# A fused attention and FFN kernel: heads' rows loaded while the chunk runs, the row sums' inverse later, input splits on two engines

## The chip, the cores and the metric

One core of a Trainium2 chip runs the kernel; the other cores do nothing. The metric is the device time of one execution in microseconds (us), as the median of several runs. TensorE is called PE here, its weight load PEld, VectorE DVE, ScalarE ACT, GpSimd POOL, and SP is the engine that only issues transfers.

## The reference

A sequence of 2048 rows of 640 numbers goes through two branches whose sum is gated row by row. Branch A is attention with 32 heads of 20 in 4 chunks of 512 rows: causal softmax inside a chunk, mixed with a read of a memory that the chunks before have filled. Branch B is a gated FFN. Abridged:

```python
g = sigmoid((x * gate_w).sum(-1, keepdims=True))
# A, for each chunk s of 4, 32 heads of 20
p = softmax(qs @ ks.T * 20 ** -0.5 + mask)
a_mem = (phi(qs) @ M) / (phi(qs) @ z + 1e-6)       # phi(t) = t + 1 if t > 0 else exp(t)
o_s = sigmoid(beta) * a_mem + (1 - sigmoid(beta)) * (p @ vs)
M, z = M + phi(ks).T @ vs, z + phi(ks).sum(rows)
a = concat(o_s) @ wo
# B
b = (silu(x @ w1) * (x @ w3)) @ w2                 # 640 -> 1728 -> 640
out = g * a + (1 - g) * b
```

Everything is float32 at the kernel's interface.

## The kernel before

**Numbers.** A float32 operand of a dense product is split into a high half (rounded to the type PE multiplies fast, `fp32r`) and a low half (what is left). `split` makes both: a copy on ACT (L111) and a subtraction on POOL, or on DVE where `lo` says so (L112). A product takes three passes: high by high, high by low, low by high. Queries and keys are cut into three bfloat16 parts each (`qs`, `ks`), which go to DRAM (`qd`, `kd`) and come back per pair of heads as `qst` and `kst`, with 120 rows.

**Attention.** `attention` is a software pipeline over 128 heads (4 chunks of 32). One step has nine places and ten ticks, called slots here. For head j, `s_unit` computes the scores three times over (s_j_0 to s_j_2), and DVE takes the row maxima under the mask (L530, result m). After every second head `max_parts` and `max_rows` cut the maxima into three bfloat16 parts and turn them (L549, result mr), and four ticks later ACT issues the transfer of mr into three more rows of `qst` (L551). Three steps behind, `st_unit` computes the transposed scores with those rows in (t_j_0 to t_j_2), ACT takes the exponential into P (tag P32, 4 buffers) and POOL masks the diagonal (L576). Four steps behind, and for four heads at once, `pv_quad` multiplies by the values (o, L587); the copy `oq` goes to DRAM as `od`, 40 slots from one quad to the next. Row 20 of a head in `od` holds its softmax sums.

**End of a chunk.** After the chunk's last quad (`q == 7`) `o_sums` loads the sums into `rs`; `o_scale` inverts them on DVE (L623 to L628: a reciprocal and five small operations that cut the result into three parts `rp`) and sends them to `rR`; `o_load` loads the heads' rows from `od` into the five blocks of `oall`. `after(n, f)` puts a call n ticks off. `normalize` multiplies: rr is a product of `rR` with a selection matrix (L649), and DVE multiplies `oall` by it and adds the memory's part `gm`.

**Dense work.** Between the attention's slots a hand-written list of jobs runs in segments: q, k and v projections, the memory's read (`memory_read`, eight halves of a product nd and four DVE operations, result gm), FFN up (g, u, result ht) and down (f, added to acc), and the output projection (op). Chunks 0 and 1 go together, then 2 and 3. `braid(a, b, every, skip)` puts one step of b after every `every` steps of a; `chain` puts jobs in a row. Weights come as raw tiles `wr` (2 buffers) and are split into `W` (6 buffers) by `w_load`, `w_split` and `w_step`, which count steps.

**What sets the order.** PE runs in the order in which the program is written. The other engines' order is made by a scheduler from a simulated time line, in which `here` and the pins hold some instructions back. Each engine works its list in order, so an instruction that waits holds everything behind it; the same goes for SP's list of transfers and for the transfers that ACT and POOL issue.

Of the kernel before, what the change touches and what calls it, by code (L numbers as in the profile page):

```python
# [8 lines left out]
F32 = mybir.dt.float32  # L9
# [8 lines left out]
P = 128  # L18
S, D, H, DH, NSEG, L = 2048, 640, 32, 20, 4, 512
F = 1728  # L20
KB = D // P
# [5 lines left out]
NST, NW, NRAW, NHT, NVG, ND = 4, 6, 2, 6, 2, 3  # L27
KR = 6 * DH
LAG_T, LAG_P, NP, AGE = 3, 4, 4, 4
HEADS = [(128 * b // DH, min(H - 1, (128 * b + 127) // DH)) for b in range(KB)]  # L30
PSEG = ((0, 512), (512, 384), (1024, 256), (896, 128))

# [2 lines left out]
def gated_mix(ctx: ExitStack, tc: tile.TileContext, xT, wqk, wv, w13, w2, w2h, wo, beta, out):  # L35
    nc = tc.nc
    cp = ctx.enter_context(tc.tile_pool(name="cp", bufs=1))
    sp = ctx.enter_context(tc.tile_pool(name="sp", bufs=2))
# [58 lines left out]
    here = tc.keep_in_program_order  # L97
    last = {}
# [11 lines left out]
    def split(dst, src, lo=None, pin=lambda ins: ins):  # L110
        pin(nc.scalar.copy(dst[:, 0], src))  # L111
        (lo or nc.gpsimd.tensor_sub)(dst[:, 1], src, dst[:, 0].bitcast(F32))  # L112
# [16 lines left out]
    items, tiles = [], {}  # L129
# [5 lines left out]
    raws, clock = [], dict(step=0, oldest=0, next=0)  # L135

    def w_load():
        k = clock["next"]
        src, n = items[k]
        raw = sp.tile([P, D + 2], F32, tag="wraw", name=f"wr{k}", bufs=NRAW)  # L140
        nc.sync.dma_start(raw[:, :n], src)
        raws.append([k, raw, n, clock["step"], None])
        clock["next"] += 1

    def w_split():
        k, raw, n, _, after = raws.pop(0)
        w = sp.tile([P, 2, D + 2], FR, tag="W", name=f"W{k}", bufs=NW)
        tiles[k] = w
        split(w[:, :, :n], raw[:, :n], lo=nc.vector.tensor_sub if k < 7 else None, pin=behind(after))

    def w_step():


        clock["step"] += 1
        for r in raws:
            if clock["step"] - r[3] == (AGE // 2 if "exp" in last else AGE) and r[0] >= 7:
                r[4] = last.get("exp", last["act"])
        if raws and raws[0][0] < clock["oldest"] + NW and \
                clock["step"] - raws[0][3] >= (AGE if "exp" in last or raws[0][0] < 7 else AGE + 1):
            w_split()  # L160
        if len(raws) < NRAW and clock["next"] < min(len(items), clock["oldest"] + NW + NRAW):
            w_load()

    def w_get(i, oldest=None):
# [9 lines left out]
    Xs, accs = {}, {}  # L174
# [14 lines left out]
    def load_wide(c):  # L189
        for kb in range(KB):  # L190
            nc.sync.dma_start(xraw[c][:, kb], xT[c, :, kb, :])
        for kb in range(KB):
            split(Xs[c][:, :, kb, :], xraw[c][:, kb])
        return
        yield

    def load_raw(c):

        if c == 2:
            wide = big_tile(f"xr{c}")  # L200
            rs = [wide[:, kb * L:(kb + 1) * L] for kb in range(KB)]
        else:
            rs = [t[:, i] for t in (ht_tile([P, 2, L], F32, f"xr{c}_{n}") for n in range(2)) for i in range(2)]
            rs.append(f_tile(f"xr{c}"))
        for kb in range(KB):
            nc.sync.dma_start(rs[kb], xT[c, :, kb, :])
        xraw[c] = rs
        return
        yield

    def split_x(c):
        x_tile(c)
        for kb in range(KB):
            split(Xs[c][:, :, kb, :], xraw[c][kb], lo=nc.vector.tensor_sub if c == 2 or kb % 2 else None, pin=here)
            yield 1

    xraw = {}
# [59 lines left out]
    def memory_read(c):  # L277
        pq = big.pop(("q", c))[:, :KB * L].rearrange("p (b n) -> p b n", b=KB)
        for qb in range(4):
            gm = ht_tile([P, D], F32, f"gm{c}_{qb}")  # L280
            for hf in range(2):
# [3 lines left out]
                for b in range(KB):  # L285
                    a0, a1 = HEADS[b]
                    u0, u1 = max(a0, 16 * hf), min(a1, 16 * hf + 15)
# [110 lines left out]
    def job_read(c):  # L398
        return 5.6, memory_read(c)

    def job_v(cs):
        iv = [w_add(wv[i], D + 2) for i in range(KB)]
        return [(17.8, v_blocks(c, iv, c == cs[-1])) for c in cs]

    def job_q(cs, mb, alloc={}):
        i = w_add(wqk[mb], D)
        return [(3.5, q_block(c, mb, i, alloc.get(c))) for c in cs]
# [173 lines left out]
    def pv_quad(j):  # L581

        ps = pp.tile([P, L], F32, tag="o", name=f"o{j}", bufs=1)
        for kb, (o, n) in enumerate(PSEG):
            for i in range(4):
                u = heads[j + i]
                nc.tensor.matmul(ps[32 * i:32 * i + 32, kb * P:], u["v"][:, kb], u["P32"][:, o:o + n],  # L587
                                 start=kb == 0, stop=kb == 3, skip_group_check=True)
        ot = sp.tile([P, L], F32, tag="oq", name=f"oq{j}", bufs=1)
        nc.scalar.copy(ot, ps)  # L590
        q = j // 4 % 8
        c, h = heads[j]["c"], heads[j]["h"]
        nc.scalar.dma_start(od[c][h:h + 4].rearrange("h e n -> (h e) n"), ot)
        if q == 7:
            after(4 if c < NSEG - 1 else 2, o_sums, c)

    turned = []

    def o_sums(c):
        here(nc.sync.dma_start(rs, od[c][:, DH].rearrange("h (a n) -> h a n", n=P)))  # L600
        after(7 if c < NSEG - 1 else 3, o_scale, c)
        for b in range(KB):
            after(1 + 6 * b if c < NSEG - 1 else 1 + b, o_load, c, b)

    def o_load(c, b):

        if b == 0:
            oall[c] = cp.tile([P, KB, L], F32, tag="oall", name=f"oall{c}", bufs=1)
        f = P * b
        queue = nc.gpsimd if c < NSEG - 1 else nc.sync  # L610
        while f < P * (b + 1):
            h, e = divmod(f, DH)
            n = min(DH - e, P * (b + 1) - f) if e else max((P * (b + 1) - f) // DH * DH, min(DH, P * (b + 1) - f))
            dst = oall[c][f - P * b:f - P * b + n, b]
            if n > DH:
                here(queue.dma_start(dst, od[c][h:h + n // DH, :DH]))
            else:
                here(queue.dma_start(dst, od[c][h, e:e + n]))
            f += n
# [42 lines left out]
    def after(n, f, *a):  # L662
        soon.append([n, f, a])
# [76 lines left out]
    def store(c, qb=None):  # L740
        o = out[0, c * L:(c + 1) * L, :].rearrange("(b p) d -> p b d", p=P)
        for qb in range(4):
            here(nc.gpsimd.dma_start(o[:, qb], accs[c][:, qb]))
            yield 1
# [12 lines left out]
    def job_down(cs, g, last=False):  # L757
        return 2.384 * sum(3 if j < NF else 2 for j in GROUPS[g]), ffn_down(cs, GROUPS[g], plan_down(GROUPS[g]), last)

    def jobs_up(cs, g):  # L760
        return [job_up(cs, j) for j in GROUPS[g]]

    def jobs_group(cs, g):
        return [job_up(cs, j) for j in GROUPS[g]] + [job_down(cs, g)]
# [14 lines left out]
    def chain(jobs):  # L779
        return sum(c for c, _ in jobs), (y for _, g in jobs for y in g)  # L780

    def braid(a, b, every, skip=0, rest=True):

        def gen():
            n = 0
            for y in a[1]:
                yield y
                n += 1
                if n > skip and (n - skip) % every == 0:
                    z = next(b[1], None)  # L790
                    if z is not None:
                        yield z
            if rest:
                yield from b[1]
        return a[0] + b[0], gen()

    A, B = (0, 1), (2, 3)
# [16 lines left out]

    seg = job_q2(A, 3)
    g = jobs_group(A, 0)
    seg += [braid(g[0], job_read(1), 2, 4)] + g[1:] + jobs_group(A, 1) + jobs_up(A, 2)
    segs.append((H + LAG_P + 1, seg))
    d = job_down(A, 2)
    u = job_up(A, GROUPS[3][0])  # L820
    o1, o2 = jobs_oproj(0)
    seg = [d, braid(u, o1, 2), o2] + [job_up(A, j) for j in GROUPS[3][1:]] + [job_down(A, 3)]
    u0, u1 = jobs_up_by_chunk(A, 4)
    seg += [(0, load_raw(2)), (0, load_raw(3))] + u0 + [braid(chain(u1), (0, split_x(2)), 3)]
    seg += [braid(job_down(A, 4), (0, split_x(3)), 3), (0, store(0))]
    seg += job_q(B[:1], 0, {2: big_tile}) + job_v(B)
    kb_, turns, writes = jobs_k(B)
    seg += kb_ + turns[:1] + job_q(B[1:], 0, {3: slot}) + turns[1:] + writes
    segs.append((2 * H - 3, seg))
    seg = job_q(B, 1) + job_q(B, 2)  # L830
    q = job_q2(B, 3)
    r = job_read(2)
    seg += q[:2] + [q[2], braid(q[3], r, 1, 0, False)]
    segs.append((2 * H + LAG_P, seg))
    up = [job_up(B, 0), job_up(B, 1)]
    o1, o2 = jobs_oproj(1)
    r = 0.37 * job_read(3)[0], chain([r, job_read(3)])[1]
    seg = [braid(braid(up[0], r, 2), (0, load_memory(1)), 5, 8), braid(up[1], o1, 2, 2), o2, (0, store(1)), job_up(B, 2), job_down(B, 0), (0, load_memory(2))] + jobs_up(B, 1)
    segs.append((3 * H + LAG_P + 1, seg))
    d = job_down(B, 1)  # L840
    u = job_up(B, GROUPS[2][0])
    o1, o2 = jobs_oproj(2)
    seg = [d, braid(u, o1, 3), o2] + [job_up(B, j) for j in GROUPS[2][1:]]
    seg += [job_down(B, 2), (0, load_memory(3))] + jobs_up(B, 3)
    segs.append((NJ + LAG_P, seg))
    d, u = job_down(B, 3), jobs_up(B, 4)
# [30 lines left out]
    while run:  # L877
# [10 lines left out]
        while credit > 0:  # L888
            d = step(run)
# [62 lines left out]
```

## Time and profile before

| | |
|---|---|
| runs | 1172.35, 1175.51, 1178.13 us; median 1175.51 |
| profiled execution | 1175.76 us, span of its instructions 1174.0 us |
| granted TensorE clock, mean | 0.995 |
| instructions | 19926 |
| DMA | 151.88 MB, mean 129 GB/s |

The page gives busy time and its share of the span for each engine, then the same in 40 slices, the transfers, and the chain of work that ended last, followed back from the last instruction. By that chain 81% of the span is PE, 7% DVE, 5% issue, 4% DMA and 2% POOL. Other views used below are the waits (who waited for whom), the windows (busy time in stretches) and the timelines. A line such as L523 is a line of the kernel before.

### The profile page before, as it was taken

The page shows a single profiled execution, that of the slowest core. Times are in us where ns is not written, and L with a number is a line of the kernel's source. Part 1 is how long each engine was busy: PE and PEld are TensorE (multiplying, and loading weights), DVE is VectorE, ACT ScalarE, POOL GpSimd, SP SyncE. Part 2 cuts the span into 40 slices and gives each one's busy share as a digit, 9 for nine tenths or more (in the row PEclk, how much of TensorE's full clock was granted, in tenths as well). Part 3 has the DMA queues.
Part 4 walks back from the last instruction along what each step waited for, and adds up shares of the span by engine and source line. Part 5 has one row for each costly group of instructions (what it writes and reads, how often), then busy time and mean ns, then how long its engine had stood idle before and what let it go on. Part 6 is the DMA issues. An engine that isn't in the chain of part 4 may idle for free.

```text
span 1174.0 us, 19926 instructions
## 1 busy us (share of the span) xinstructions
PE 1147.3 (98%) x6953; PEld 873.1 (74%) x6953; DVE 676.9 (58%) x2116; ACT 487.7 (42%) x924; POOL 494.6 (42%) x636
## 2 busy tenths in 40 slices
PE   8999999999999999999999988999999999999998
PEld 5978866767767787878876655767768776776888
DVE  5043575466656653674255886866567676663444
ACT  6255344544343234253365633445543344344130
POOL 7065533244245335254175544343445325344250
PEclk9999999999999999999999998999999999999999
DMA  8365733322324225225376865242434324231212
GB/s 282 121 212 208 242 102 94 94 89 83 89 94 131 69 83 152 89 74 178 117 248 222 251 204 162 84 152 91 151 107 127 97 67 134 73 117 53 82 58 90
DMA packets 108097, 151.88 MB, mean 129 GB/s; under 512 B 14244, under 2 KB 71588, under 8 KB 107996
## 3 DMA queue, kind: packets, MB, share of 16 engines
q1 hardware_dynamic: 80908, 112.71, 30.9%
q10 hardware_dynamic: 22080, 27.40, 6.6%
q0 software_dynamic: 5008, 10.50, 2.8%
q8 instruction: 54, 0.88, 0.3%
q14 instruction: 47, 0.39, 0.1%
HBM read 95.25 MB, written 54.53 MB: 128 GB/s over the span
## 4 chain that ended last, share of the span: by engine, by line
PE 81%; DVE 7%; issue 5%; DMA 4%; POOL 2%; ACT 1%; POOLq 0%; SPq 0%; ACTq 0%; DVEq 0%
PE f L478 15%; PE u L225 14%; PE g L225 14%; PE o L587 6%; PE s L523 6%; PE k L225 5%; PE q L225 5%; PE op L724 4%; PE t L562 4%; PE v L325 3%; DVE junk L530 2%; DMA wr<-in_wqk_dram 2%; PE pm L381 1%; PE t L567 1%; DMA od<-oq 1%
## 5 line engine op out<-in xcount | busy, mean ns | idle before, releaser
L530 DVE CUSTOM_DVE_ANT_0 junk<-s,mask 128x128 bf16<-128x128 f32 (+3 forms) x512 | 249.4, 487 | 202.0 <-PE s L523 193.0
L570 ACT ACTIVATE P<-t 128x384 f32<-128x384 f32 (+1 forms) x384 | 201.8, 527 | 343.8 <-PE t L562 106.9
L112 POOL TENSOR_TENSOR W<-wr,W 128x640 fp32r<-128x640 f32 (+1 forms) x126 | 197.6, 1573 | 232.5 <-ACT W L111 224.6
L576 POOL TENSOR_SCALAR_AFFINE_SELECT P<-P 128x256 f32<-128x256 f32 x256 | 106.8, 419 | 329.2 <-ACT P L570 328.6
L225 PE MATMUL g<-X,W 128*128 128x512 f32 x840 | 242.5, 424 | 0.1
L225 PE MATMUL u<-X,W 128*128 128x512 f32 x780 | 228.4, 427 | 0.6 <-DVE oall L650 0.6
L478 PE MATMUL f<-W,ht 128*128 128x320 f32 x1312 | 223.9, 321 | 2.9 <-DVE ft L453 2.2
L478 PEld LDWEIGHTS f<-W,ht 128*128 128x128 f32 x1312 | 199.6, 189 | 10.5 <-DVE ft L453 2.7
L225 PEld LDWEIGHTS g<-X,W 128*128 128x128 f32 x840 | 152.3, 190 | 27.4 <-issue 2.6
L225 PEld LDWEIGHTS u<-X,W 128*128 128x128 f32 x780 | 143.2, 192 | 29.6 <-issue 5.4
L523 PE MATMUL s<-kst,qst 120*128 120x128 bf16 (+3 forms) x512 | 135.6, 305 | 5.2 <-DVE m L530 5.2
L111 ACT CAST W<-wr 128x640 fp32r<-128x640 f32 (+1 forms) x133 | 95.3, 726 | 100.4 <-PE f L478 26.1
L483 DVE SCALAR_TENSOR_TENSOR acc<-f,cgate,acc 128x320 f32<-128x320 f32 x128 | 69.7, 549 | 56.8 <-PE f L478 55.8
L562 PE MATMUL t<-qst,kst 123*128 123x512 bf16 (+1 forms) x256 | 93.5, 365 | 4.9 <-DMA qst<-mr 4.8
L112 POOL TENSOR_TENSOR ht<-ft,ht 128x512 fp32r<-128x512 f32 x52 | 66.9, 1287 | 52.3 <-ACT ht L111 52.3
L225 PE MATMUL q<-X,W 128*128 128x512 f32 x300 | 81.9, 418 | 3.1 <-POOL X L112 1.9
L523 PEld LDWEIGHTS <-qst 120*128 120x128 bf16 x512 | 45.0, 99 | 52.4 <-issue 44.3
L724 PE MATMUL op<-W,oT 128*128 128x320 f32 x480 | 82.3, 323 | 0.0
L225 PE MATMUL k<-X,W 128*128 128x512 f32 x300 | 80.2, 411 | 1.1 <-ACT mt L385 1.1
L587 PE MATMUL o<-P,vg 128*32 128x512 f32 (+3 forms) x1024 | 77.3, 441 | 0.1
L325 PE MATMUL v<-W,X 128*128 128x320 f32 (+1 forms) x480 | 75.9, 317 | 0.0
L724 PEld LDWEIGHTS op<-W,oT 128*128 128x128 f32 x480 | 73.7, 190 | 1.5
(114 smaller groups left out, 1250.0 us busy)
## 6 DMA issues: line engine op xcount, KB each, us to landing
wr<-in_w_dram SPq DMA_DIRECT2D x80, 320.0 KB
qst<-qd SPq DMA_DIRECT2D x64, 240.0 KB
kst<-kd SPq DMA_DIRECT2D x64, 240.0 KB
od<-oq ACTq DMA_DIRECT2D x32, 256.0 KB
qd<-qs ACTq DMA_DIRECT2D x20, 384.0 KB
kd<-ks SPq DMA_DIRECT2D x20, 384.0 KB
wr<-in_wqk_dram SPq DMA_DIRECT2D x21, 320.0 KB
wr<-in_wo_dram SPq DMA_DIRECT2D x20, 320.0 KB
```

Source lines behind the costliest of these rows:

```text
L111: pin(nc.scalar.copy(dst[:, 0], src))
L112: (lo or nc.gpsimd.tensor_sub)(dst[:, 1], src, dst[:, 0].bitcast(F32))
L225: nc.tensor.matmul(ps, w[:, a, kb * P:(kb + 1) * P], x[:, b, kb, :], start=n == 0, stop=n == 14)
L325: nc.tensor.matmul(ps[:, :n1 - n0], x[:, a, kb, lb * P:(lb + 1) * P], wvt[kb][:, b, n0:n1], start=n == 0, stop=n == 14)
L478: nc.tensor.matmul(ps[:, :320], a, b, start=n == 0, stop=n == len(ms) - 1)
L523: nc.tensor.matmul(ps[:, o:o + n], q[:KR, qb * P:(qb + 1) * P], k[:KR, :n], start=qb != 1, stop=qb != 0, skip_group_check=True)
L530: nc.vector.tensor_tensor_reduce(out=junk[:, :n], in0=ps[:, o:o + n], in1=mask[:, L - n:], scale=1.0, scalar=-3.0e38, op0=ALU.add, op1=ALU ...
L562: nc.tensor.matmul(ps[:, :n], k[:KR + 3, t * P:(t + 1) * P], q[:KR + 3, t * P:], start=True, stop=True)
L570: last["exp"] = nc.scalar.activation(P32[:, o:o + n], src, AF.Exp, scale=SCALE)
L576: nc.gpsimd.affine_select(d, d, pattern=[[0, 2], [1, P]], base=0, channel_multiplier=-1, compare_op=ALU.is_ge, fill=0.0)
L587: nc.tensor.matmul(ps[32 * i:32 * i + 32, kb * P:], u["v"][:, kb], u["P32"][:, o:o + n], start=kb == 0, stop=kb == 3, skip_group_check=True)
L724: nc.tensor.matmul(ps[:, :320], oT[0][:, qb % 2, a, kb * P:(kb + 1) * P], ws[kb][:, b, 320 * hf:320 * hf + 320], start=n == 0, stop=n == 14)
```

## The change

It does five things. The heads' rows are loaded block by block after quads 4, 5 and 6 of a chunk (two blocks after the last of these), 8 ticks after each, and only the last block after the sums; in the last chunk too, where those loads move from SP to POOL. The sums are loaded 6 ticks after the last quad (4 before) and inverted 16 ticks later (7 before), except in the last chunk. The low halves of X1, X2 and X3 are shared by POOL and DVE in turn (before: X1 on POOL, X2 on DVE, X3 in turn), and the splits of X2 and X3 are spread over more jobs. Weights 2 to 5 are loaded at the head into P's tiles, which are free then, at fixed steps; weights' splits wait two steps longer before attention. The memory's reads are spread: of chunk 1 over the first two FFN up jobs, of chunk 2 over the last two q jobs, with four of eight halves and not five ahead of the segment's end.

```diff
+EARLY = range(2, 6)
+OUT = {4: (0,), 5: (1,), 6: (2, 3)}
...
     def w_load():
-        raw = sp.tile([P, D + 2], F32, tag="wraw", name=f"wr{k}", bufs=NRAW)
+        if k in EARLY:
+            raw = sp.tile([P, 1280], F32, tag="P32", name=f"wr{k}", bufs=NP)
+        else:
+            raw = sp.tile([P, D + 2], F32, tag="wraw", name=f"wr{k}", bufs=NRAW)
...
     def w_step():
-            if clock["step"] - r[3] == (AGE // 2 if "exp" in last else AGE) and r[0] >= 7:
+            if clock["step"] - r[3] == (AGE // 2 if "exp" in last else AGE + 2) and r[0] >= 7:
...
-        if raws and raws[0][0] < clock["oldest"] + NW and \
-                clock["step"] - raws[0][3] >= (AGE if "exp" in last or raws[0][0] < 7 else AGE + 1):
+        if raws and raws[0][0] in EARLY:
+            if clock["step"] >= 6 + 2 * raws[0][0]:
+                w_split()
+        elif raws and raws[0][0] < clock["oldest"] + NW and \
+                clock["step"] - raws[0][3] >= (AGE if "exp" in last or raws[0][0] < 7 else AGE + 3):
             w_split()
-        if len(raws) < NRAW and clock["next"] < min(len(items), clock["oldest"] + NW + NRAW):
+        if sum(r[0] not in EARLY for r in raws) < NRAW and clock["next"] < min(len(items), clock["oldest"] + NW + NRAW):
             w_load()
...
     def load_wide(c):
             nc.sync.dma_start(xraw[c][:, kb], xT[c, :, kb, :])
+        for _ in EARLY:
+            w_load()
         for kb in range(KB):
-            split(Xs[c][:, :, kb, :], xraw[c][:, kb])
+            split(Xs[c][:, :, kb, :], xraw[c][:, kb], lo=nc.vector.tensor_sub if kb % 2 else None)
...
     def split_x(c):
-            split(Xs[c][:, :, kb, :], xraw[c][kb], lo=nc.vector.tensor_sub if c == 2 or kb % 2 else None, pin=here)
+            split(Xs[c][:, :, kb, :], xraw[c][kb], lo=nc.vector.tensor_sub if kb % 2 else None, pin=here)
...
     def pv_quad(j):
+        for b in OUT.get(q, ()):
+            after(8, o_load, c, b)
         if q == 7:
-            after(4 if c < NSEG - 1 else 2, o_sums, c)
+            after(6 if c < NSEG - 1 else 2, o_sums, c)
...
     def o_sums(c):
-        after(7 if c < NSEG - 1 else 3, o_scale, c)
-        for b in range(KB):
-            after(1 + 6 * b if c < NSEG - 1 else 1 + b, o_load, c, b)
+        after(16 if c < NSEG - 1 else 3, o_scale, c)
+        if c == NSEG - 1:
+            o_load(c, KB - 1)
+        else:
+            after(6, o_load, c, KB - 1)
...
     def o_load(c, b):
-        queue = nc.gpsimd if c < NSEG - 1 else nc.sync
+        queue = nc.gpsimd if (c, b) != (NSEG - 1, KB - 1) else nc.sync
...
-    seg += [braid(g[0], job_read(1), 2, 4)] + g[1:] + jobs_group(A, 1) + jobs_up(A, 2)
+    seg += [braid(chain(g[:2]), job_read(1), 3, 4)] + g[2:] + jobs_group(A, 1) + jobs_up(A, 2)
...
-    seg += [(0, load_raw(2)), (0, load_raw(3))] + u0 + [braid(chain(u1), (0, split_x(2)), 3)]
-    seg += [braid(job_down(A, 4), (0, split_x(3)), 3), (0, store(0))]
-    seg += job_q(B[:1], 0, {2: big_tile}) + job_v(B)
+    x2, x3 = split_x(2), split_x(3)
+    seg += [(0, load_raw(2)), (0, load_raw(3))] + u0 + [braid(chain(u1), (0, x2), 4, 0, False)]
+    d = job_down(A, 4)
+    q = job_q(B[:1], 0, {2: big_tile})
+    seg += [braid(chain([braid(d, (0, x2), 4), (0, store(0))] + q), (0, x3), 4, 6)] + job_v(B)
...
-    seg += q[:2] + [q[2], braid(q[3], r, 1, 0, False)]
+    seg += q[:2] + [braid(chain(q[2:]), r, 2, 2, False)]
```

In the built programs the change shows in the order of the engines other than PE above all. Numbers behind a name are buffers; lines of the changed kernel lie 2 to 16 further down.

DVE at the turn from chunk 1 to chunk 2, before: `rs` is the sums' tile, `junk` and `m68` the maximum of a score tile of heads 68 and 69, `nd_r` part of a memory read, `fu2_0` of the FFN.

```order
L447 SCALAR_TENSOR_TENSOR fu2_0_7630<-ft2_0_7629,g2_0_7521 128x512
L623 RECIPROCAL rs_101<-rs_101 128x128
L530 ISA junk_7654,m68_7330<-s68_2_7652,mask_89 128x512
L530 ISA m68_7330 128x1
L296 TENSOR_SCALAR nd_r_7660<-nd2_3_1_7656 128x16
L624 TENSOR_SCALAR rs_101<-rs_101,cR_99 128x128
L530 ISA junk_7684,m68_7330<-s69_0_7681,mask_89 128x128
L530 ISA m68_7330 128x1
L297 RECIPROCAL nd_r_7660<-nd_r_7660 128x16
L625 CAST rp_102<-rs_101 128x128
```

And in the changed kernel:

```order
L540 ISA junk_7699,m68_7342<-s69_1_7697,mask_89 128x384
L540 ISA m68_7342 128x1
L463 SCALAR_TENSOR_TENSOR ft2_0_7620<-fu2_0_7621,u2_0_7632 128x512
L637 RECIPROCAL rs_101<-rs_101 128x128
L540 ISA junk_7723,m68_7342<-s69_2_7721,mask_89 128x512
L540 ISA m68_7342 128x1
L306 TENSOR_SCALAR nd_r_7740<-nd3_0_0_7736 128x16
L638 TENSOR_SCALAR rs_101<-rs_101,cR_99 128x128
L550 CAST ns0_104<-m68_7342 128x8
L307 RECIPROCAL nd_r_7740<-nd_r_7740 128x16
L639 CAST rp_102<-rs_101 128x128
L551 TENSOR_TENSOR nm_7725<-m68_7342,ns0_104 128x8
```

The inverse has moved from ahead of s68_2 to behind s69_1, so its small operations now lie among those that make `ns` and mr of heads 68 and 69.

POOL in the same stretch, before; the transfers fill chunk 1's `oall`.

```order
L576 AFFINE_SELECT P63_7433<-P63_7433 128x2x128
L112 TENSOR_TENSOR W82_7525<-wr82_7185,W82_7525 128x640
L616 DMA oall1_7587<-od1_81 120x1x512
L618 DMA oall1_7587<-od1_81 8x512
L576 AFFINE_SELECT P63_7433<-P63_7433 128x256
L261 TENSOR_TENSOR qs3_4_7476<-qs3_4_t_7481,qs3_4_7476 128x512
L505 MEMSET vg72_7677 128x4x12
L618 DMA oall1_7587<-od1_81 4x512
L616 DMA oall1_7587<-od1_81 120x1x512
L618 DMA oall1_7587<-od1_81 4x512
L576 AFFINE_SELECT P64_7513<-P64_7513 128x2x128
```

And in the changed kernel, where blocks 2 and 3 stand ahead of P61 (block 0 stands behind P52, block 1 behind P56, block 4 behind P64):

```order
L586 AFFINE_SELECT P60_7193<-P60_7193 128x2x128
L586 AFFINE_SELECT P60_7193<-P60_7193 128x256
L632 DMA oall1_6451<-od1_81 4x512
L630 DMA oall1_6451<-od1_81 120x1x512
L632 DMA oall1_6451<-od1_81 4x512
L632 DMA oall1_6451<-od1_81 16x512
L630 DMA oall1_6451<-od1_81 100x1x512
L632 DMA oall1_6451<-od1_81 12x512
L271 TENSOR_TENSOR qs2_3_7253<-qs2_3_t_7258,qs2_3_7253 128x512
L586 AFFINE_SELECT P61_7290<-P61_7290 128x2x128
```

Four of the five blocks have left the stretch behind P63; they now wait on POOL for the quads that wrote them.

POOL at the head, before: X1 is chunk 1's input, all five low halves on POOL.

```order
L112 TENSOR_TENSOR X1_110<-xr1_111,X1_110 128x512
L311 MEMSET V0_317 128x128
L112 TENSOR_TENSOR X1_110<-xr1_111,X1_110 128x512 x2
L261 TENSOR_TENSOR qs0_0_184<-qs0_0_t_186,qs0_0_184 128x512
L112 TENSOR_TENSOR X1_110<-xr1_111,X1_110 128x512 x2
L261 TENSOR_TENSOR qs0_1_242<-qs0_1_t_244,qs0_1_242 128x512
```

And in the changed kernel; the other two are on DVE, behind the low half of W2:

```order
L321 MEMSET V0_317 128x128
L114 TENSOR_TENSOR X1_110<-xr1_111,X1_110 128x512 x2
L271 TENSOR_TENSOR qs0_0_192<-qs0_0_t_194,qs0_0_192 128x512
L114 TENSOR_TENSOR X1_110<-xr1_111,X1_110 128x512
L321 MEMSET V1_473 128x128
L271 TENSOR_TENSOR qs0_1_235<-qs0_1_t_237,qs0_1_235 128x512
```

POOL is through with X1 after three subtractions, one q part earlier than before.

## Prediction

> **What bounds the kernel now.** I read the page's engine table first, then its row of granted clock over 40 slices, the waits of PE, the windows around the largest of them, and last the chain and the timelines of the engines that PE waits for.
>
> ```profile
> PE 1147.3 (98%) x6953; PEld 873.1 (74%) x6953; DVE 676.9 (58%) x2116; ACT 487.7 (42%) x924; POOL 494.6 (42%) x636
> PEclk9999999999999999999999998999999999999999
> ```
>
> PE's waits, by what it waited for (us in total, times, longest):
>
> ```profile
> PE s L523 <- DVE m L530: 5.2, 6, 3.0
> PE t L562 <- DMA qst<-mr: 4.8, 1, 4.8
> PE f L478 <- DVE ft L453: 2.2, 2, 1.3
> PE k L225 <- ACT mt L385: 1.1, 1, 1.1
> ```
>
> PE is busy for 98% of the span, so the change can only win back idle time of PE and time at a low clock; it removes no matmul. The clock falls in one slice of 40, number 25 (from about 704 us), so I looked there first. The four waits shown are 13.3 us. Single stretches of the dip:
>
> ```profile
> 672.00:692.00 20.00, 18.86 (x129) 12.73 (x127) 19.26 (x75) 9.32 (x19) 12.25 (x19) 1.00 0.77 243
> 692.00:720.00 28.00, 19.96 (x115) 12.78 (x115) 15.01 (x62) 5.65 (x11) 9.74 (x16) 0.82 0.52 160
> 720.00:744.00 24.00, 23.73 (x159) 15.84 (x155) 20.51 (x75) 9.87 (x19) 7.90 (x13) 1.00 0.35 109
> ...
> 696.00:700.00 4.00, 1.13 (x3) 0.94 (x3) 2.69 (x13) 0.00 (x0) 0.00 (x0) 0.81 0.56 155
> 700.00:704.00 4.00, 4.00 (x21) 2.65 (x20) 3.86 (x15) 1.50 (x3) 0.81 (x2) 0.77 0.34 111
> 712.00:716.00 4.00, 1.65 (x4) 1.03 (x4) 0.00 (x0) 0.00 (x0) 0.91 (x2) 0.51 1.02 328
> 716.00:720.00 4.00, 4.00 (x35) 1.29 (x34) 0.56 (x2) 0.00 (x0) 0.00 (x0) 0.63 0.07 28
> ```
>
> After the window's length come PE, weight loads, DVE, ACT, POOL, the granted clock, the DMA share. This is the turn from chunk 1 to chunk 2. PE idles 28 - 19.96 = 8.04 us in the middle stretch. Where the clock is short it is at half: (0.19 + 0.23) x 4 x 2 = 3.4 us around 700, with PE busy about 3.0 of it, and (0.49 + 0.37) x 4 x 2 = 6.9 us around 715, with PE busy about 4.6. Half of that busy time is lost: 1.5 + 2.3 = 3.8 us. How it came about:
>
> ```profile
> 687.13 6.41 DMA od<-oq
> 697.31 0.95 DVE L623 RECIPROCAL rs<-rs 128x128 f32<-128x128 f32 x1 [4.63 <-DMA rs<-od]
> 698.87 0.48 PE L523 MATMUL s<-kst,qst 120*128 120x384 bf16 x1 [3.05 <-DVE m L530]
> 701.98 0.39 PE L523 MATMUL s<-kst,qst 120*128 120x512 bf16 x1
> 703.18 0.68 DVE L530 CUSTOM_DVE_ANT_0 junk<-s,mask 128x512 bf16<-128x512 f32 x1
> 707.90 6.40 DMA qst<-mr
> 714.35 0.61 PE L562 MATMUL t<-qst,kst 123*128 123x512 bf16 x1 [4.81 <-DMA qst<-mr]
> ...
> 750.24 1.94 DMA qst<-mr
> ```
>
> The last quad of chunk 1 lands in od at 693.5, its row sums in rs at 697.3. DVE had come to the reciprocal 4.63 us before and stood there, with the maxima of the next scores behind it, so PE stood 3.05 us. Late maxima gave a late mr, whose transfer took 6.40 us beside the row loads, and PE stood 4.81 us more.
>
> **The change, part by part.** (a) The reciprocal. The row-sum load is put off from 4 to 6 slots after the quad, the inverse from 7 to 16 after that. On DVE it moves from ahead of s68_2 to behind s69_1 and ft2_0, as the rows of the order show: the maxima of s68_2, s69_0 and s69_1 (0.68 us and less, about 2.2 together), ft (another 0.6) and two halves of the memory read now run first, some 5 us of DVE work. That covers the 4.63. On SP the row-sum load stands in the queue until od has landed, with the next heads' loads behind it; two slots later it stands there less. The 3.05 goes (ends: 0 and -3.05; I take -3.05) and the clock loss behind it, -1.5 (0 to -1.5).
>
> (b) The second stall. The six DVE operations of the inverse now stand in the chain from s69_2 to mr, or right ahead of it:
>
> ```profile
> L628 DVE TENSOR_TENSOR rp<-rs,rp x4: 281/289/1328, 375.0 to 1099.7; 128x128 bf16<-128x128 f32 x4
> ```
>
> In the trace mr left 707.90 - 703.18 = 4.72 us after DVE began s69_2's maximum, and DVE began 1.2 us after PE's row. Five operations of 0.29 or less add about 1.3: 7.2 us. From s69_2 to where t68_0 would have started PE needs 714.35 - 4.81 - 701.98 = 7.56 us. That leaves 0.4 us for the transfer, which takes between 1.94 (quiet) and 6.40 (DMA share about 1). Of the five blocks of rows, which POOL issued behind P63 to P66, four now come before P61 and the last behind P64, so less is under way and I put it at 2.4, nearer the quiet row: the wait falls from 4.81 to 2.0, -2.8 (ends: +1.2 with 6.4 us, and -4.81). A wait under 3.05 should not halve the clock: -2.3 (0 to -2.3). [...]
>
> (c) DVE's load there. The same work is 19.26 + 15.01 + 20.51 = 54.8 us from 672 to 744, and PE at full clock without its 9.45 us of idle needs 72 - 9.45 - 3.8 = 58.8: DVE is 93% loaded. One of the memory-read halves goes ahead of 672, but DVE also loses its rest during the stall (0.56 us busy in 712 to 720). From 672 to 692, at 96%, PE lost 6% (1.14 of 20). At 4% of 58.8 PE loses 2.4 us in small waits, where it now loses 9.45 - 3.05 - 4.81 = 1.6 beside the two stalls: +0.8 (from -1.6 to +1.9).
>
> (d) Head: X1's low halves shared.
>
> ```profile
> 16.04 3.71 POOL L112 TENSOR_TENSOR X<-xr,X 128x512 fp32r<-128x512 f32 x2
> 9.63 0.69 DVE L112 TENSOR_TENSOR X<-xr,X 128x512 fp32r<-128x512 f32 x1 [0.22 <-ACT X L111]
> 17.96 0.96 PE L225 MATMUL q<-X,W 128*128 128x512 f32 x3 [1.03 <-POOL X L112]
> 19.80 4.20 PE L225 MATMUL q<-X,W 128*128 128x512 f32 x17 [0.87 <-POOL X L112]
> 23.84 35.85 PE L325 MATMUL v<-W,X 128*128 128x320 f32 x240
> ```
>
> POOL's last pair runs to 19.75, and PE waits 1.03 + 0.87. Two of five go to DVE at 0.69; POOL does three and is through near 16. The wait goes: -1.9 (0 to -1.9). The early loads of four weights into P's tiles gain nothing by themselves: all 240 v matmuls ran without a wait. They stand behind X1's loads on SP, so they delay nothing that PE waits for (0; up to +1, the 0.87 again, if X1 came late).
>
> (e) to (h), smaller places. Rows of the timelines (start, length, instruction, in brackets the idle time ahead of it and what ended it) and three of the chain:
>
> ```profile
> 72.81 0.72 ACT L111 CAST W<-wr 128x640 fp32r<-128x640 f32 x1 [2.31 <-DMA wr<-in_wqk_dram]
> 149.98 0.96 PE L291 MATMUL nd<-Ms,pq 128*128 128x84 f32 x6 [0.71 <-DVE gm L299]
> 161.13 0.38 PE L523 MATMUL s<-kst,qst 120*128 120x512 bf16 x1 [0.56 <-DVE m L530]
> 371.10 0.95 DVE L623 RECIPROCAL rs<-rs 128x128 f32<-128x128 f32 x1 [2.17 <-DMA rs<-od]
> 374.22 2.92 PE L478 MATMUL f<-W,ht 128*128 128x320 f32 x18 [0.86 <-DVE ft L453]
> 396.89 0.23 PE rr L649
> 399.14 2.29 PE o L587 x32
> 444.27 2.29 PE o L587 x32
> 519.15 1.29 POOL L112 TENSOR_TENSOR X<-xr,X 128x512 fp32r<-128x512 f32 x1
> 519.23 1.24 DVE L542 CAST ns<-nm 128x8 bf16<-128x8 f32 x1
> 521.33 1.00 PE L478 MATMUL f<-W,ht 128*128 128x320 f32 x5 [1.32 <-DVE ft L453]
> ```
>
> (e) In the k blocks a cast on ACT, for a weight needed much later, waits 2.31 for its load with mt's copy behind it. The later split puts it behind mt but ahead of the next k copy: half of PE's 1.1 us, -0.5 (0 to -1.1). (f) Chunk 1's memory read is spread over two FFN blocks instead of one: half of 0.71 + 0.56, -0.7 (0 to -1.3). (g) At the turn from chunk 0 DVE waits 2.17 and PE 0.86; the inverse moves behind ft: -0.8 (0 to -0.9). The inverse comes 2 + 9 slots later; two quads, 40 slots apart, start 45.1 us apart here, so that is about 12 us, and the inverse ends near 387. Its first reader, rr, stands at 396.9, and rR's three loads, now behind one weight load on SP, have 9 us to land: 0. (h) X2's low halves go from DVE alone to DVE and POOL, X3's later: DVE saves one of 0.69 ahead of ft, but POOL's X still lies beside it, and beside such a one a cast took 1.24: -0.5 (0 to -1.3). [...] (i) The early row loads on POOL, the last chunk's among them (formerly SP's): the same number of issues, covered by POOL's idle time (58%); 0, but see the third rival. One memory read moves over a segment's border, which shifts PE's later rows by a step without adding any; 0 either way. PE's rows at the end are the same.
>
> The sum: -3.05 - 1.5 - 2.8 - 2.3 + 0.8 - 1.9 - 0.5 - 0.7 - 0.8 - 0.5 = -13.25 us. The profiled execution took 1175.76 us (span 1174.0 and 1.76 around it), so 1162.5; the median of the three runs, 1175.51, lies 0.25 below it.
>
> **The rivals.** First: t68_0 still waits whole. Its slack of 0.4 us speaks for it, the removed row loads against. The wait of 4.81 and the half clock behind it stay: 1162.5 + 2.8 + 2.3 = 1167.6.
>
> Second: the turn is bound by DVE, and the stalls only changed their name. For it speaks the 93%; against it, that PE lost only 0.27 us from 720 to 744 at 85%. Then (a) to (c), 8.85 us, are not won: 1171.4, which is no change.
>
> Third, slower: the row loads of quads 4 to 6 block POOL's queue.
>
> ```profile
> 854.71 2.29 PE o L587 x32
> 877.40 2.29 PE o L587 x32
> ```
>
> Quads are 22.7 us and 40 slots apart, so the load comes 8 x 0.57 = 4.5 us after its quad, while od took 6.41 us to land in a busy stretch. POOL may so stand some 2 us at each of 12 places (three quads of four chunks), with P's masks, the weights' and ht's low halves behind it. That the masked tiles are read only when their own quad comes, up to 22.7 us later, speaks against it. It decides from 13.25 + 5.9 = 19.15 us, or 1.6 us of PE at each place: 1175.76 + 5.9 = 1181.7 and more.
>
> **How the numbers follow.** The forecast has 0.68, the rivals 0.18, 0.09 and 0.05. A change of under 0.5% (5.9 us) can't be told from none: the three runs alone lie that far apart. Faster: 0.68 + 0.18, less 0.03 for the part of the first rival that falls short of 1169.6: 0.83; same 0.09 + 0.03 = 0.12; slower 0.05. The range: every term at its best gives -19.8 us or 1156.0, which needs all of them at once, and I stop at 1157; above, it takes in the first rival with 2.6 us for small waits: 1170. The second and third, 0.14, are left out.
>
> **What will show it.** (a) is right if DVE has no wait for rs of over 0.5 us at the turns of chunks 0 and 1, wrong if one of 2 us is there. (b) if PE's longest wait for mr is under 3 us and the clock row has no low slice. (c) if PE's waits for DVE from 670 to 735 are 2 to 3 us in all. (d) if PE waits no more for POOL X and v starts near 22 instead of 23.8. (f) to (h) by the three rows above. What would make it wrong: a new stall of 3 us or more at the turn, with a half clock behind it, or POOL waiting for od with PE behind it.

## The result and the profile after

| | before | changed |
|---|---|---|
| runs (us) | 1172.35 to 1178.13, median 1175.81 | 1162.19 to 1163.30, median 1163.26 |
| ratio | | 0.9893, 95% interval 0.9868 to 0.9919 |
| profiled execution, span | 1175.76, 1174.0 | 1163.27, 1161.6 |

The forecast was 1162.5. The page of the changed kernel, its engine table and its row of granted clock, and then the largest of PE's waits behind its first matmuls (total, times, longest):

```profile
PE 1142.8 (98%) x6953; PEld 872.6 (75%) x6953; DVE 674.8 (58%) x2115; ACT 487.3 (42%) x924; POOL 499.6 (43%) x648
PEclk9999999999999999999999999999999999999999
```

```profile
PE t L572 <- DMA qst<-mr: 3.1, 3, 1.7
PE s L533 <- DVE m L540: 1.7, 4, 0.6
PE k L235 <- ACT mt L395: 1.2, 2, 1.0
PE f L488 <- DVE ft L463: 1.1, 1, 1.1
PE nd L301 <- DVE gm L309: 1.1, 2, 0.7
```

The low slice of the clock is gone and no wait is over 1.7 us. Single rows of the turn and of the places where PE now waits, from the timelines:

```profile
375.88 0.94 DVE L637 RECIPROCAL rs<-rs 128x128 f32<-128x128 f32 x1
693.17 0.94 DVE L637 RECIPROCAL rs<-rs 128x128 f32<-128x128 f32 x1
699.41 0.76 ACTq L561 DMA_DIRECT2D qst<-mr  x1
701.52 0.39 PE L572 MATMUL t<-qst,kst 123*128 123x512 bf16 x1
21.33 4.89 PE L335 MATMUL v<-W,X 128*128 128x320 f32 x32
```

DVE does not wait for rs at the turns of chunks 0 and 1 (no bracket), mr of heads 68 and 69 is there after 2.11 us instead of 6.40, t68_0 starts without a wait of its own, and v starts at 21.33 instead of 23.84. The windows of the turn (length, then PE, weight loads, DVE, ACT, POOL, clock, DMA share):

```profile
664.00:684.00 20.00, 18.70 (x127) 12.95 (x125) 17.38 (x64) 10.98 (x21) 9.77 (x14) 1.00 0.83 273
684.00:712.00 28.00, 26.91 (x179) 19.08 (x179) 23.90 (x105) 11.15 (x22) 10.84 (x18) 1.00 0.62 180
712.00:740.00 28.00, 26.71 (x165) 17.07 (x164) 23.41 (x79) 11.93 (x23) 8.56 (x15) 1.00 0.38 110
```

PE idles 76 - 72.32 = 3.7 us there in small waits, all of them for DVE. PE's lead, the start of the same PE row in the trace of before less that in the trace of the changed kernel:

| place | before | changed | lead |
|---|---|---|---|
| after the k blocks | 113.57 | 110.66 | 2.91 |
| after chunk 1's read | 200.19 | 196.50 | 3.69 |
| after the turn from chunk 0 | 374.62 | 369.79 | 4.83 |
| before t58_0 | 644.91 | 639.36 | 5.55 |
| after t58_0 | 645.60 | 641.33 | 4.27 |
| before chunk 1's turn | 679.54 | 675.26 | 4.28 |
| after it | 734.74 | 721.06 | 13.68 |
| after t80_0 | 785.18 | 772.93 | 12.25 |
| last matmul | 1169.99 | 1157.30 | 12.69 |

So 9.40 us come from the turn, 5.5 from the small places and the head, and two new waits, at t58_0 and t80_0, take back 1.3 and 1.4.

### The profile page after: what moved, and what is told of

Read it like the earlier page. It is cut to its first block, busy times and chain, and to the rows that moved or that the text cites. A ratio compares the mean times of both kernels' runs of the same rounds, so it can differ in the third digit from the quotient of the medians.

```text
span 1161.6 us, 19926 instructions
## 1 busy us (share of the span) xinstructions
PE 1142.8 (98%) x6953; PEld 872.6 (75%) x6953; DVE 674.8 (58%) x2115; ACT 487.3 (42%) x924; POOL 499.6 (43%) x648
## 4 chain that ended last, share of the span: by engine, by line
PE 88%; DVE 6%; DMA 2%; issue 2%; ACT 1%; POOL 0%; SPq 0%; POOLq 0%; ACTq 0%; DVEq 0%
PE f L488 16%; PE g L235 16%; PE u L235 15%; PE o L597 6%; PE v L335 6%; PE s L533 6%; PE q L235 5%; PE k L235 5%; PE op L738 4%; PE t L572 4%; DVE junk L540 1%; PE pm L391 1%; PE nd L301 1%; PE t L577 1%; DMA qst<-mr 1%
## 5 line engine op out<-in xcount | busy, mean ns | idle before, releaser
L235 PE MATMUL u<-X,W 128*128 128x512 f32 x780 | 225.9, 425 | 0.6 <-DVE nd_r L306 0.6
```

Of the source, the lines that this page charges most:

```text
L235: nc.tensor.matmul(ps, w[:, a, kb * P:(kb + 1) * P], x[:, b, kb, :], start=n == 0, stop=n == 14)
```

## The experiments

Three edits touch the turn: the inverse put off (I), the rows early (R), chunk 2's memory read spread (M). The rest (head, chunk 1's read, weights' steps, splits of X2 and X3, the last chunk's rows) is called H.

| run | has | median, range (us) | ratio to before, interval |
|---|---|---|---|
| changed | I R M H | 1163.26, 1162.19 to 1163.30 | 0.9893, 0.9868 to 0.9919 |
| e1 | I M H | 1165.49, 1165.25 to 1167.43 | 0.9916, 0.9901 to 0.9931 |
| e2 | R M H | 1164.34, 1164.22 to 1164.63 | 0.9903, 0.9888 to 0.9918 |
| e3 | M H | 1166.73, 1165.49 to 1167.18 | 0.9924, 0.9908 to 0.9941 |
| e6 | I R H | 1164.84, 1163.04 to 1166.09 | 0.9906, 0.9891 to 0.9921 |
| e9 | H | 1170.79, 1169.10 to 1171.57 | 0.9959, 0.9945 to 0.9972 |
| b1 | I | 1172.98, 1169.72 to 1176.95 | 0.9980, 0.9967 to 0.9993 |
| b2 | R | 1165.02, 1164.31 to 1166.77 | 0.9914, 0.9897 to 0.9932 |
| b3 | M | 1168.92, 1167.51 to 1170.18 | 0.9941, 0.9922 to 0.9961 |
| e12 | R H | 1159.82, 1159.41 to 1161.51 | 0.9880, 0.9862 to 0.9898 |
| e13 | R H, later block | 1160.12, 1159.44 to 1161.96 | 0.9880, 0.9864 to 0.9896 |
| e5 | all, X1's low halves on POOL | 1165.56, 1163.47 to 1166.08 | 0.9921, 0.9904 to 0.9937 |
| e4 | all, no early weights | 1164.28, 1163.67 to 1166.37 | 0.9916, 0.9899 to 0.9933 |

The kernel before ran beside each set: 1175.62 beside e1 to e6, 1175.58 beside e9 to b3, 1173.54 beside the last four.

**e1, rows late.** In the changed kernel:

```diff
-        for b in OUT.get(q, ()):
+        for b in OUT.get(q, ()) if c == NSEG - 1 else ():
...
-            after(6, o_load, c, KB - 1)
+            for b in range(KB):
+                after(1 + 6 * b, o_load, c, b)
```

> The changed kernel with the row loads of chunks 0 to 2 put back behind the last quad (POOL issues them 1, 7, 13, 19, 25 ticks after the sums' load); the inverse stays put off. Theory A (two causes: the inverse made the first stall, the row loads beside mr the second): no PE wait of 3 us for the maxima of s69, but mr of heads 68 and 69, which leaves about 6.8 us after s69_2, takes 5 to 6.4 us again where it took 2.11, so PE waits 3.5 to 5 us at t68_0 and may lose 0 to 2.3 us more to a half clock; the wait of 1.11 us at t58_0, beside block 0's load, goes. Time 1163.3 + 3.5 to 5 + 0 to 2.3 - 1.1 = 1165.7 to 1169.5. Theory B (the inverse alone was the cause, the second stall only its echo): no wait over 1 us at t68_0, time 1162 to 1163.5.

The wait came back, with a half clock behind it (mean granted clock 0.997 in e1, 1.000 in the changed kernel), but smaller than expected:

```profile
697.81 0.76 ACTq L561 DMA_DIRECT2D qst<-mr  x1
703.00 0.39 PE L572 MATMUL t<-qst,kst 123*128 123x512 bf16 x1 [2.68 <-DMA qst<-mr]
```

The transfer took 5.2 us where it took 2.11. The wait at t58_0 was gone. Theory B falls.

**e2, inverse early.**

```diff
-            after(6 if c < NSEG - 1 else 2, o_sums, c)
+            after(4 if c < NSEG - 1 else 2, o_sums, c)
...
-        after(16 if c < NSEG - 1 else 3, o_scale, c)
+        after(7 if c < NSEG - 1 else 3, o_scale, c)
```

> The changed kernel with the sums' load 4 ticks after the last quad and the inverse 7 ticks after that, as before; the rows stay early. Theory A: od still lands some 6 us after its quad and the sums 3 to 4 us later, so DVE stands 3 to 5 us at the reciprocal in the turn from chunk 1, PE waits 2 to 3 us for maxima with about 1.5 us of half clock, and 0.9 us at the turn from chunk 0; mr of heads 68 and 69 stays near 2 us and t68_0 waits under 1 us. Time 1163.3 + 2 to 3 + 0 to 1.5 + 0.9 = 1166 to 1168.7. Theory C (the row loads alone were the cause: with them gone the sums land in time): DVE's wait for rs is under 1 us, time 1163 to 1164.5.

Theory A was wrong here. With the rows early, DVE hardly stands at the early inverse:

```profile
687.91 0.95 DVE L637 RECIPROCAL rs<-rs 128x128 f32<-128x128 f32 x1 [0.71 <-DMA rs<-od]
```

So it was the row loads that had made the sums late, as theory C says.

**e3, both.**

> Both of the above: the end of a chunk as before, the rest (head, memory reads, splits) as changed. Theory A: the two stalls and the half clocks come back, which were 9.5 us in the trace from 676 to 720, and 1.1 us at the turn from chunk 0; the wait at t58_0 (1.11) goes: 1163.3 + 9.5 + 1.1 - 1.1 = 1172.8, and the two single undoings need not add up, since a late mr is worse beside the rows. If the rest of the change had carried more than it seems, the time would be under 1169.

6 us better than expected: DVE stood 3.06 us for rs where it had stood 4.63, PE lost 0.60, 0.67 and 0.49 in place of 3.05, and mr took 3.2 us. Something outside I and R carried part of the turn.

**e6, chunk 2's read as before.**

```diff
-    seg += q[:2] + [braid(chain(q[2:]), r, 2, 2, False)]
+    seg += q[:2] + [q[2], braid(q[3], r, 1, 0, False)]
```

> The changed kernel with chunk 2's memory read as before (one half after each step of the last q job, five of eight halves ahead of the segment's end). Theory A: the new PE wait of 1.69 us at t80_0 comes from PE's order, which now has three matmuls less (27 and not 30 dense ones, 1.3 us) between s81_2 and t80_0 and so asks for mr earlier; with the old order it is under 0.5 us, and the turn loses 0 to 1 us to DVE. Time 1163.3 - 1.4 + 0 to 1 = 1161.9 to 1162.9. Rival: the wait comes from the transfer or from DVE and stays over 1 us; time 1163.3 or more.

Half right. The wait at t80_0 is gone, so PE's order made it. But t68_0 waits again, although the rows are early:

```profile
693.89 1.22 DVE L639 CAST rp<-rs 128x128 bf16<-128x128 f32 x1
699.56 0.75 ACTq L561 DMA_DIRECT2D qst<-mr  x1
703.46 0.61 PE L572 MATMUL t<-qst,kst 123*128 123x512 bf16 x1 [3.28 <-DMA qst<-mr]
```

mr left 7.45 us after s69_2 (at 692.11; 6.86 in the changed kernel, 5.92 before): the put-off inverse lies in its chain, as the prediction's step (b) had it. Its transfer took 3.90 us, and no row load was beside it, but 0.82 MB of another queue's loads (packets, MB, share of the 16 engines from 699.56 to 703.46; in the changed kernel 0.05 MB on that queue beside mr):

```profile
q1 hardware_dynamic: 657, 0.82, 68.2%
```

**e9, all three undone.** The diffs of e1, e2 and e6 together.

> The changed kernel with all three edits that touch the turn from chunk 1 undone: inverse early, rows late and chunk 2's memory read as before; only the head, chunk 1's memory read, the weights' steps and the splits of X2 and X3 stay changed. Theory D (the two stalls are one chain, and any of the three edits breaks most of it, so the single undoings add up to less than the whole): both stalls come back with their half clocks, PE waits 2 us or more for maxima and 3 us or more at t68_0. The head and the small places are 2.74 + 0.16 + 0.79 + 0.7 = 4.4 us by PE's lead in the traces, so 1175.6 - 4.4 = 1171.2, from 1170 to 1173. If the edits were independent, the undoings would add: 1166.7 + 1.6 = 1168.3 or less.

1170.8, and both stalls are back:

```profile
697.09 0.48 PE L533 MATMUL s<-kst,qst 120*128 120x384 bf16 x1 [3.11 <-DVE m L540]
711.50 0.39 PE L572 MATMUL t<-qst,kst 123*128 123x512 bf16 x1 [2.44 <-DMA qst<-mr]
```

The second is shorter than expected. H is worth 4.8 us, and the three edits of the turn 7.5 together, while e1, e2 and e6 lose 2.2, 1.1 and 1.6 (4.9): they overlap.

**b1, b2, b3: one edit alone, in the kernel before.** The same lines as above, the other way round: b1 has 6 and 16 ticks, b2 `OUT` for chunks 0 to 2 and the last block 6 ticks after the sums' load, b3 the braid over `q[2:]`.

> The kernel before with the inverse alone put off (sums' load 6 ticks after the last quad, inverse 16 after that). By the prediction's step (a) DVE no longer stands for rs and PE's 3.05 with its 1.5 of half clock and 0.9 at the turn from chunk 0 go; by its step (b) the inverse's small operations then lie in mr's chain, mr leaves 6.6 to 7.4 us after s69_2 and takes 5 to 6.4 us beside the rows, so the wait at t68_0 stays at 4 to 6 us with its half clock: 1175.6 - 3.05 - 1.5 - 0.9 + 0 to 1 = 1170.2 to 1171.2. Theory D's strongest form (the first stall is what makes the second): the second goes as well, 1175.6 - 9.65 - 0.9 = 1165.

> The kernel before with the row loads of chunks 0 to 2 alone put early (blocks 0 to 3 behind quads 4 to 6, the last 6 ticks after the sums' load). Step (b) of the prediction alone: t68_0's wait of 4.81 falls to 0 to 1 and its 2.3 of half clock goes, while the first stall of 3.05 with 1.5 stays: 1175.6 - 4.3 - 2.3 + 1.1 (the new wait at t58_0 beside block 0) = 1170.1. Theory D: od and the sums land sooner too, DVE stands under 2.5 us, PE's first stall is under 1 us and keeps its clock: another 2 + 1.5 less, 1166.6.

> The kernel before with chunk 2's memory read alone spread over the last two q jobs (four halves ahead of the segment's end in place of five). The prediction gave this edit nothing. With inverse and rows as before it was worth 1171.2 - 1166.7 = 4.5 us in the changed kernel, if that estimate of the rest holds: 1175.6 - 4.5 = 1171.1, with DVE's wait for rs near 3 us, PE's first stall 1 to 1.5 us in place of 3.05, t68_0's wait under 1.5 in place of 4.81, and a new wait of 1 to 1.7 us at t80_0. By the prediction's step: 1175.6.

b1 gains 2.6 us, less than either theory said. DVE did not stand, but mr left 7.98 us after s69_2 and t68_0 waited longer than before:

```profile
705.54 0.76 ACTq L551 DMA_DIRECT2D qst<-mr  x1
711.53 0.61 PE L562 MATMUL t<-qst,kst 123*128 123x512 bf16 x1 [5.91 <-DMA qst<-mr]
```

b2 gains 10.6 us, more than theory D said: no stall is left at the turn (DVE stands 0.59 us for rs, PE 0.19 at t68_0). Three rows of b2's chain that ended last, then the same of before (od's row of before stands in the prediction), b3, e9 and e12 (start, time to landing, transfer):

```profile
686.60 3.81 DMA od<-oq
690.42 2.35 DMA rs<-od
702.89 1.93 DMA qst<-mr
```

```profile
693.56 3.73 DMA rs<-od
```

```profile
688.09 6.04 DMA od<-oq
694.15 2.41 DMA rs<-od
705.65 3.64 DMA qst<-mr
```

```profile
685.29 6.45 DMA od<-oq
691.76 3.75 DMA rs<-od
706.48 4.97 DMA qst<-mr
```

```profile
681.61 3.89 DMA od<-oq
685.52 2.32 DMA rs<-od
```

SP's load of the sums waits for od, so every trace gives od's time. At this turn it is 6.0 to 6.5 us in before, e3, e9 and b3, and 3.2 to 4.0 in the eight traces with the rows early. But it is as short in b1 (issued at 686.44, 3.95) and e1 (3.81), where the rows are late:

```profile
690.41 0.55 SPq L600 DMA_DIRECT2D rs<-od  x1
```

The late row loads count from the sums' load, so I alone puts them off by two ticks as well, and most of them then come behind od. What moved on POOL's queue, q0, during od, in before, b1 and b2 (packets, MB, share of the 16 engines):

```profile
q0 software_dynamic: 631, 0.76, 40.0%
q0 software_dynamic: 231, 0.08, 19.4%
q0 software_dynamic: 18, 0.01, 2.7%
```

In the four slow traces it was 0.60 to 0.76 MB, in the ten others at most 0.13: od was late for the row loads. So b1 is not the inverse alone; it also took the row loads off od. The row loads lie beside mr too (5.2 us in e1), but other loads alone also stretch it (3.90 in e6).

b3 gains 6.7 us where the prediction gave that edit 0 and the estimate was 4.5. There od is nearly as slow as before (6.04), but the sums' load takes 2.41 us and not 3.73. Beside it in before lay a load that POOL issues for the memory's read; in b3 that load comes behind the sums (before, then b3):

```profile
693.44 0.59 POOL L640 DMA_DIRECT2D gm<-gd  x1 [0.63 <-PE nd L291]
697.20 0.59 POOL L640 DMA_DIRECT2D gm<-gd  x1 [0.19 <-PE t L562]
```

It is the same in e9 (3.75, the load beside it) and e3 (2.58, behind it). The shift also gives PE three more dense matmuls (36, 33 before) between the last quad and s69_0, and again three (36, 33) from s69_2 to t68_0, so it asks later for what was late. How much of the 6.7 us each of these carries was not isolated.

**e12, e13: the rows and H, without the other two.** e2's and e6's diffs together; e13 also has:

```diff
-            after(8, o_load, c, b)
+            after(18 if b == 0 else 8, o_load, c, b)
```

> The changed kernel with the inverse early and chunk 2's memory read as before, but the row loads early: the edit that alone gave 10.6 us at the turn, beside the head and the small places. Theory E (the late row loads were the common root: they lay beside the last quad's od, its sums and mr; with them gone the other two edits cost more than they win, since the put-off inverse lies in mr's chain and the shifted read brings t80_0's wait of 1.69): 1165.0 - (1175.6 - 1170.8 = 4.8) = 1160.2, from 1159.5 to 1161.5, that is 2 to 3 us faster than the changed kernel. If the two edits help beside the rows as their single undoings say (1.1 and 1.6 us), the time is 1163.3 + 2.7 = 1166.

> The same with block 0 loaded 18 and not 8 ticks after quad 4. Theory: the new wait at t58_0 (1.11 us in the changed kernel, 0.85 in the one with the rows alone) is block 0's load, whose issue on POOL and transfer lie beside the chain to mr of heads 58 and 59; moved off, it goes: 0.8 to 1.1 us less than the run before, near 1159.3. If the wait comes from DVE's load there, it stays and so does the time.

e12 came out as theory E says. Its page and its turn:

```profile
PE 1142.2 (99%) x6953; PEld 872.5 (75%) x6953; DVE 676.2 (58%) x2115; ACT 486.2 (42%) x924; POOL 499.7 (43%) x648
```

```profile
684.00:712.00 28.00, 27.33 (x180) 19.14 (x179) 23.84 (x106) 11.28 (x21) 10.71 (x19) 1.00 0.58 184
712.00:740.00 28.00, 27.71 (x172) 18.46 (x171) 23.95 (x77) 13.19 (x25) 10.75 (x16) 1.00 0.37 111
```

PE idles 1157.7 - 1142.2 = 15.5 us over the span, 18.8 in the changed kernel; t80_0 has no wait for mr. By medians e12 is 3.4 us faster than the changed kernel, and no run of one reaches the other's. By the ratios to before, whose runs beside e12 were faster, it is about 1.5 us, and the intervals overlap. The two were not run in one set, so its lead is put at 1.5 to 3.4 us.

e13 changed nothing (the wait at t58_0 was 0.77, 0.53 in e12). The expectation named the wrong block: the loads beside mr of heads 58 and 59 come 8 ticks after quad 5, so they are block 1's, and e13 left them there. That the rows make this wait rests on e1, where it vanished: the eight traces with the rows early have it (0.37 to 1.32 us), the six with the rows late do not; which block's, or whether POOL's issue or the transfer, is open.

**e5, e4: the head.** e5 takes `lo` out of `load_wide`, e4 sets `EARLY = ()`.

> The changed kernel with all low halves of X1 on POOL again; the early weight loads stay. By the prediction's step (d) the shared low halves carry the whole lead of the head: PE waits 1.9 us for POOL X again and v starts 1.9 to 2.7 us later, 1165.2 to 1166. If the early loads carry it, v starts less than 0.5 us later and the time is 1163.3 to 1163.8.

> The changed kernel without the early loads of weights 2 to 5; the shared low halves stay. By step (d) the early loads gain nothing by themselves: v starts within 0.3 us of 21.1 and the time is 1163.0 to 1163.6. If they carry what the head won beyond 1.9 (its lead was 2.74), v starts 0.8 us later and the time is 1164.1.

PE's rows of e5, then of e4:

```profile
17.82 0.97 PE L235 MATMUL q<-X,W 128*128 128x512 f32 x3 [1.11 <-POOL X L114]
19.63 4.21 PE L235 MATMUL q<-X,W 128*128 128x512 f32 x17 [0.84 <-POOL X L114]
23.68 1.04 PE L335 MATMUL v<-W,X 128*128 128x320 f32 x6
```

```profile
21.55 1.64 PE L335 MATMUL v<-W,X 128*128 128x320 f32 x10
24.30 0.41 PE L335 MATMUL v<-W,X 128*128 128x320 f32 x1 [0.31 <-ACT W L113]
25.36 0.85 PE L335 MATMUL v<-W,X 128*128 128x320 f32 x4 [0.65 <-DVE W L114]
```

The shared halves carry v's start, as step (d) said. But without the early loads v waits for its weights, 0.96 us in two waits: the early loads are what lets v follow a q that ends sooner.

## Why the prediction was right, and where it was not

The time was right, the causes of the largest terms only in part. In the order of its steps:

- **(a), the reciprocal, -4.55.** DVE's wait went, but the step put the whole wait down to the inverse's place. b2 removes it with the inverse where it was; b1 puts the inverse off and gains 2.6 us in all, and even there the row loads had moved off od. The step that failed is that it took od's 6.41 us as given and did not ask what lay beside it: POOL's row loads.
- **(b), the second stall, -5.1.** The mechanism was right in part: mr left 6.86 us after s69_2 (forecast 7.2) and took 2.11 (forecast 2.4), and with the row loads beside it 5.2 (e1). But by the step's own 7.56 us of PE the wait would still be 6.86 + 2.11 - 7.56 = 1.4. It is 0 because PE took 8.97 us from s69_2 to t68_0: there are the three more dense matmuls of the memory read's shift, which the sum put at nothing, and a wait of 0.63 for DVE's nd_r. With the inverse put off but without the shift t68_0 waits 3.28 (e6). That I makes mr later was right too, and is one reason why I alone is worth so little and why e12 does without it.
- **(c), small waits, +0.8.** 3.7 us of waits for DVE from 664 to 740 where 2 to 3 were forecast. (a) to (c) were 8.85 together and measured 9.40.
- **(d), the head, -1.9, and (e), the k blocks, -0.5.** 2.91 together. The shared halves are right (e5); the early loads, forecast 0, hold about 1 us of it (e4): they covered a wait that the sum did not see, since v as it stood then did not wait. (e) itself won nothing: a k block still waits 1.0.
- **(f), (g), (h): -0.7, -0.8, -0.5.** 0.78, 1.14 and 0.72, as PE's lead grew over each place (the last from after the turn from chunk 0 to before t58_0). But of the 0.72 only 0.18 was won at the wait that (h) had read, 1.32 in the prediction's row:

```profile
516.34 1.00 PE L488 MATMUL f<-W,ht 128*128 128x320 f32 x5 [1.14 <-DVE ft L463]
```

Another 0.30 is a wait of f for acc (at 531.42 before) that is gone and that the sum did not have.

- **The memory read's shift, forecast 0, "either way".** This step failed. It added to PE's work ahead of t68_0, as (b) says, and took as much from that ahead of t80_0. In its place stands t80_0's wait: between s81_2 and t80_0 PE has 27 dense matmuls where it had 30 (the order of the rows in the two traces), so it asks for mr some 1.1 us sooner after s81_2, and waits 1.69. e6 shows it, and b3 that the same edit helps the turn.
- **(i), the early rows, forecast 0.** They cost 1.28 us at t58_0.

The terms that were too small (1.7 us in all), 0.4 us won behind t80_0 that no term names, and the two waits that were not in the sum (2.7) nearly cancel; that the result is within 0.8 us of the forecast is partly luck.

Of the rivals, the first (t68_0 waits whole) and the second (DVE takes the turn back) did not come. Nor did the third: POOL stood for od once in the changed kernel, at 686.76, for the block loaded behind the chunk's last quad and not behind quads 4 to 6, and no PE wait came of it:

```profile
POOL oall L630 <- DMA od<-oq: 1.5, 1, 1.5
```

## What to carry to other kernels

When an engine stands for a transfer, look first at what else is on the DMA engines during that transfer, and only then at where the waiting instruction stands: moving bulk loads away from the few small transfers on the critical path did more here (10.6 us in b2) than putting off the instruction that waited (2.6 in b1). Several edits at one stall overlap, so take each alone and each away before keeping all; beside the early rows the other two together won nothing. A shift of PE's order by a step is not free where a transfer lands just in time: t80_0 came to wait 1.69 us for mr.

## What the runs showed of the hardware

**Where the clock fell.** In the trace of before it is at half for 3.41 us from 698.46 and for 6.83, twice that, from 712.11, which is four times 3.41 later; the stretch at the end, from 1172.91, starts 460.8 us or 135 such lengths after that. So these stretches start on one grid of 3.41 us. Windows on it:

```profile
695.05:698.46 3.41, 0.77 (x7) 0.64 (x6) 1.15 (x2) 0.60 (x1) 0.00 (x0) 1.00 0.83 240
698.46:701.87 3.41, 3.00 (x8) 1.95 (x7) 3.38 (x20) 0.49 (x1) 0.24 (x1) 0.50 0.17 56
708.70:712.11 3.41, 0.84 (x5) 0.35 (x3) 2.63 (x12) 1.70 (x3) 2.05 (x3) 1.00 0.80 235
712.11:715.53 3.42, 1.18 (x3) 1.03 (x4) 0.00 (x0) 0.00 (x0) 0.80 (x2) 0.50 1.06 335
715.53:718.94 3.41, 3.41 (x19) 0.82 (x21) 0.56 (x2) 0.00 (x0) 0.00 (x0) 0.50 0.19 74
```

Windows of the same length from e1, and from e4 (counted back there from its one stretch, at the end):

```profile
772.49:775.90 3.41, 1.59 (x10) 1.04 (x10) 2.16 (x9) 2.60 (x5) 2.28 (x3) 1.00 0.90 320
775.90:779.31 3.41, 3.41 (x17) 1.13 (x19) 0.57 (x2) 0.00 (x0) 2.58 (x4) 0.50 0.82 233
```

```profile
769.90:773.31 3.41, 1.58 (x10) 0.78 (x8) 2.49 (x9) 2.60 (x5) 1.90 (x3) 1.00 0.84 312
773.31:776.72 3.41, 2.77 (x25) 1.29 (x29) 0.62 (x4) 0.00 (x0) 2.95 (x5) 1.00 0.88 230
```

In e1 PE idles 1.82 us in one window, and the next runs at half clock. In e4 it idles 2.47 over two, 1.83 of it in the first, and the clock stays. In the traces of before and of the changed kernel, full-clock windows on the grid behind the first 12 us with up to 1.31 us of idle time were followed by full clock, those with 2.57 or more by half. That a wait under 3.05 us keeps the clock was an estimate of the prediction, from its one wait of that length; e1's 1.82 us did not keep it, while e4's 2.47 did. What decided between these two is open.
